# Linear attention and token mixing on one core: a new order table, eps added by TensorE, VectorE work moved away, and 26 products on constant data

## The chip, the cores and the metric

The kernel runs on one core of a Trainium2 chip. The metric is the device time of one execution in microseconds (us). The span of a profile, from the first to the last instruction, is about 2 us shorter. (The profiled execution of the first kernel took 130.3 us, which is 1.8 us over its span; against its median the difference is 3.3 us, as this execution was a quick one.) A run is called slow when it is over 1.5% above the fastest run of the same kernel, otherwise fast; only fast runs are compared. PSUM is the memory that takes TensorE's results here, in banks, and an evacuation is a copy out of it. The granted clock is the share of its full clock that TensorE got, as the profile records it.

## The reference, cut to what matters

```python
# q, k, v: 8 batches x 8 heads x 576 positions x 64, fp32
phi(x) = concat(relu(x) * cos(pos), relu(x) * sin(pos))        # 64 -> 128 features
kv, z  = sum_s phi(k) v^T, sum_s phi(k)                        # per head
x      = phi(q) kv / (phi(q) z + 1e-6)                         # normalization
# x is 8 x 576 x 512 (heads side by side)
W      = (x w_q)(x w_k)^T / 8                                  # 576 x 576 per batch
out    = relu(W x) w_out                                       # 8 x 576 x 512
```

## The kernel before

Every step is a small function. A table, ORDER, lists some 690 words of the form operation.arguments@engine, and the program issues them in that order. Each engine is given its own words in table order. T is TensorE with a PSUM bank, V VectorE (DVE in the profile), A ScalarE (ACT), G GpSimd (POOL), Y SyncE (SP), which issues the transfers.

```python
N_RAW, N_RK, N_KP, N_QD, N_VB, N_QPT, N_KV = 4, 2, 3, 3, 3, 4, 4     # buffers of each kind
N_XS, N_XT, N_WQK, N_WKJ, N_KX, N_MIX, N_OSB = 3, 2, 2, 2, 2, 2, 6
EPS_PE = False
# LD  load half of head pair H (two groups, so four heads) of q, k or v
#         RK, CV, DQ  relu of k, cast of v, doubled relu of q
# MK  kp = rk * cossin (VectorE)                 QK  kv products and q transposes of one group of two heads
# EK  kvs <- PSUM    EQ  qpt <- PSUM * cst       NM  numerators and denominators
def RC(eng, pb, g):
    den = num_view(at["NM", g])[:, :, :, D:D + 1]
    if EPS_PE:
        eng.reciprocal(rec[g % 4], den)
    else:
        eng.tensor_scalar_add(rec[g % 4], den, EPS)
        eng.reciprocal(rec[g % 4], rec[g % 4])
# XN  xs = numerator * rec (the normalization)   XT, WQK, TK, KX, MX  transposes and mixing of one batch
def EO(eng, pb, b, t):                             # evacuation of one output tile
    n, ts = unit_of[b, t]
    copy(eng, osb[n % N_OSB][:, ts.index(t), :], bank1(at["WO", b, t], 0, 4 * DM, FP32))
def ST(eng, pb, b, u, hi):                         # store of one finished output buffer
    ...                                            # (cut: offsets)
    eng.dma_start(dst, osb[n % N_OSB][64 * hi:64 * hi + 64, 0:len(ts), :])
```

There are 32 groups, so 32 normalizations; they serve as landmarks below. WO is the output projection: 36 tiles of four products each.

## Time and profile before

| | before |
|---|---|
| time, median | 131.8 us |
| span of the profile | 128.5 us |
| busy: TensorE, VectorE, ScalarE, GpSimd | 105.4, 106.2, 77.5, 69.4 us |
| end of the 8th, 24th and 32nd normalization | 37.3, 84.6, 108.6 us |
| end of TensorE | 122.2 us |

The ends of normalizations are read from the timeline of VectorE, by counting the multiplications that write xs. Busy shares are averages over stages with different limits, so they have to be read by stretch; the prediction shows these lines. One more line belongs to it, from the waits of SyncE's queue of the kernel before (what it waited for; us in total, times, longest):

```profile
SPq L208 <- ACT rk L193: 8.6, 1, 8.6
```

### The profile page before, as it was taken

The numbers are of one execution on the slowest core, as the hardware profiler recorded it, in microseconds if no ns is written. First come the engines' busy times: TensorE is split into PE (matmuls) and PEld (weight loads), VectorE is DVE, ScalarE is ACT, GpSimd is POOL, SyncE is SP. The second block draws the span as 40 slices with busy tenths as digits, with TensorE's granted clock in tenths as the row PEclk, the third lists the DMA queues.
The fourth block names the chain that finished last, engine by engine and source line by source line (L and its number), as shares of the span: only waits on it lengthen the run. The fifth ranks groups of instructions, "written<-read, shape, count | busy, mean of one in ns | idle before, by whom it ended". The sixth has DMA issues, their size and how long they took to land.

```text
span 128.5 us, 5197 instructions
## 1 busy us (share of the span) xinstructions
PE 105.4 (82%) x2198; PEld 69.4 (54%) x2198; DVE 106.2 (83%) x227; ACT 77.5 (60%) x124; POOL 69.4 (54%) x81
## 2 busy tenths in 40 slices
PE   5935594887879979878999969889999999999900
PEld 2314584847667546566676557364576775543400
DVE  3466999987899999999999896999999998774600
ACT  7125443966396698974976758647977655147110
POOL 7009817098969979995078252389949740020000
PEclk9995558655799999999999999999999999999995
DMA  4999999999999999992068999999998799468793
GB/s 133 276 389 406 391 391 390 331 392 388 389 387 392 391 385 391 390 386 103 5 146 319 303 360 363 340 329 403 384 377 309 176 341 248 107 197 278 186 289 100
DMA packets 20711, 39.40 MB, mean 307 GB/s; under 512 B 3280, under 2 KB 3280, under 8 KB 20688
## 3 DMA queue, kind: packets, MB, share of 16 engines
q1 hardware_dynamic: 19152, 36.32, 81.8%
q10 hardware_dynamic: 1536, 2.75, 6.1%
q8 instruction: 17, 0.28, 0.9%
q14 instruction: 6, 0.05, 0.1%
HBM read 29.62 MB, written 9.44 MB: 304 GB/s over the span
## 4 chain that ended last, share of the span: by engine, by line
DVE 31%; PE 30%; POOL 10%; DMA 8%; SPq 7%; issue 6%; ACT 3%; ACTq 2%; POOLq 0%
DVE kp L232 10%; PE banks L413 10%; DVE xs L309 8%; DVE qpt L279 7%; POOL qd L195 5%; PE banks L260 5%; SPq L208 5%; DMA qf<-in_q_dram 5%; PE banks L269 4%; DMA vf<-in_v_dram 4%; PE banks L292 3%; SPq L430 2%; DVE rec L305 2%; PE banks L343 2%; POOL vb L189 2%
## 5 line engine op out<-in xcount | busy, mean ns | idle before, releaser
L195 POOL TENSOR_SCALAR qd<-qf 128x1152 bf16<-128x1152 f32 x32 | 39.1, 1231 | 12.7 <-DMA qf<-in_q_dram 11.6
L413 PE MATMUL banks<-wo_sb,mix 128*128 128x512 bf16 x144 | 36.0, 380 | 0.0
L232 DVE TENSOR_TENSOR kp<-rk,cossin 128x1152 bf16<-128x1152 bf16 x32 | 29.2, 932 | 1.4 <-POOL rk L195 1.3
L185 ACT COPY osb<-banks 128x512 f32<-128x512 f32 x31 | 18.0, 589 | 12.9 <-PE banks L413 8.2
L309 DVE TENSOR_TENSOR xs<-banks,rec 128x640 bf16<-128x640 f32 x32 | 25.4, 808 | 0.3
L279 DVE TENSOR_TENSOR qpt<-banks,cst 128x1152 bf16<-128x1152 bf16 x32 | 23.9, 746 | 1.1 <-PE banks L269 0.8
L401 ACT ACTIVATE mix<-banks 128x640 bf16<-128x640 f32 (+1 forms) x27 | 17.4, 656 | 8.7 <-PE banks L388 8.1
L260 PE MATMUL banks<-vb,kp 64*128 64x65 bf16 x576 | 16.7, 202 | 3.8 <-DVE kp L232 1.8
L413 PEld LDWEIGHTS <-mix 128*128 128x128 bf16 x144 | 12.1, 98 | 12.5 <-issue 1.4
L292 PE MATMUL banks<-kvs,qpt 128*128 128x65 bf16 x320 | 16.2, 203 | 3.1 <-DVE kvs L187 2.2
L269 PE MATMUL banks<-ident,qd 64*128 64x64 bf16 x576 | 16.2, 201 | 2.2 <-POOL qd L195 2.2
L292 PEld LDWEIGHTS <-qpt 128*128 128x128 bf16 x320 | 13.8, 103 | 7.1 <-DVE qpt L279 2.5
L260 PEld LDWEIGHTS <-kp 64*128 64x128 bf16 x576 | 13.6, 100 | 7.2 <-DVE kp L232 2.5
L193 ACT ACTIVATE rk<-kf 128x576 bf16<-128x576 f32 x15 | 10.1, 684 | 9.1 <-DMA kf<-in_k_dram 8.9
L195 POOL TENSOR_SCALAR rk<-kf 128x576 bf16<-128x576 f32 x14 | 11.3, 812 | 6.6 <-DMA kf<-in_k_dram 2.8
L189 POOL TENSOR_SCALAR vb<-vf 128x576 bf16<-128x576 f32 x17 | 12.3, 726 | 4.6 <-DMA vf<-in_v_dram 3.5
L269 PEld LDWEIGHTS <-qd 64*128 64x128 bf16 x576 | 12.9, 102 | 2.4 <-POOL qd L195 2.4
L185 ACT COPY xT<-banks 128x1280 bf16<-128x1280 bf16 x10 | 12.2, 1225 | 2.9 <-PE banks L326 2.9
L185 ACT CAST vb<-vf 128x576 bf16<-128x576 f32 x14 | 9.4, 673 | 4.7 <-DMA vf<-in_v_dram 4.5
L326 PE MATMUL banks<-ident,xs 64*128 64x64 bf16 x320 | 7.8, 196 | 4.2 <-DVE xs L309 4.1
L189 POOL TENSOR_SCALAR wq<-wqk 64x576 bf16<-64x576 bf16 x4 | 2.8, 712 | 14.9 <-DVE wqk L187 7.8
L343 PE MATMUL banks<-xT,wqk_sb 128*128 128x288 bf16 x64 | 10.1, 306 | 0.7 <-DVE xs L309 0.3
(46 smaller groups left out, 112.8 us busy)
## 6 DMA issues: line engine op xcount, KB each, us to landing
kf<-in_k_dram SPq DMA_DIRECT2D x32, 288.0 KB, 6.0
vf<-in_v_dram SPq DMA_DIRECT2D x32, 288.0 KB, 5.9
qf<-in_q_dram SPq DMA_DIRECT2D x32, 288.0 KB, 6.0
out_dram<-osb SPq DMA_DIRECT2D x21, 256.0 KB, 4.4
out_dram<-osb ACTq DMA_DIRECT2D x9, 256.0 KB, 4.3
out_dram<-osb SPq DMA_DIRECT2D x9, 128.0 KB, 3.4
wo_f<-in_moe_w_out_dram SPq DMA_DIRECT2D x1, 1024.0 KB, 8.3
out_dram<-osb ACTq DMA_DIRECT2D x3, 128.0 KB, 4.0
```

The lines of the kernel that those rows point to most:

```text
L185: A.copy(dst, src)
L189: eng.tensor_scalar(dst, src, 1.0, 1.0, op0=ALU.mult, op1=ALU.mult)
L195: eng.tensor_scalar(dst, src, FMAX, 0.0, op0=ALU.min, op1=ALU.max)
L232: eng.tensor_mul(kp[H % N_KP][:, lo:hi], rk[H % N_RK][:, lo:hi].unsqueeze(3).to_broadcast([P, n, C9, 2, D]), cossin.unsqueeze(1).to_broadc ...
L260: T.matmul(kvp[:, hh, :], kp[H % N_KP][p0:p0 + 64, i, c, :, :], vb[H % N_VB][p0:p0 + 64, i, c, 0:D + 1], start=(c == 0), stop=(c == C9 - 1))
L269: T.transpose(qt[:, hh, c * D:(c + 1) * D], src, ident[p0:p0 + 64, p0:p0 + 64])
L279: eng.tensor_mul(qpt[g % N_QPT][:, :, 1:SLOTS, :], qk_views(at["QK", g])[0].rearrange("f h (c d) -> f h c d", c=C9), cst.unsqueeze(1).to_b ...
L292: T.matmul(nv[:, hh, u, :], qpt[g % N_QPT][:, hh, 2 * u:2 * u + 2, :], kvs[g % N_KV][:, hh, :], start=(u == 0), stop=(u == SC - 1 and not ...
L309: eng.tensor_tensor(xs[b % N_XS][:, :, 2 * pr:2 * pr + 2, :].rearrange("p u h d -> p h u d"), num_view(at["NM", g])[:, :, :, 0:D], rec[g % ...
L343: T.matmul(w[:, nh, :], wqk_sb[:, dmc, :], xT[b % N_XT][:, dmc, D + nh * HS:D + (nh + 1) * HS], start=(dmc == 0), stop=(dmc == NDM - 1))
L401: A.activation(dst, src, AF.Relu, scale=scale_moe)
L413: T.matmul(o, mix[b // 2 % N_MIX][:, dmc, base:base + P], wo_sb[:, dmc, :], start=(dmc == 0), stop=(dmc == NDM - 1))
```

## The change

The intent was to relieve VectorE. The denominators get their eps inside PSUM from a tiny TensorE product, so that 32 VectorE additions go. Thirty of 32 kvs copies go from VectorE to ScalarE, k-relus and v casts from ScalarE and VectorE to GpSimd, ten of the twelve stores that ScalarE issued to SyncE, and more output copies from VectorE to ScalarE. Ten words WU put 26 products on constant data into early gaps of TensorE, to keep its granted clock up. The whole table was rearranged.

```diff
-EPS_PE = False
+EPS_PE = True
+    def WU(eng, pb, n):
+        for _ in range(n):
+            T.matmul(bank1(pb, 0, 2048, FP32), warm[:, 0:P], warm, start=True, stop=True)
 # NM, with EPS_PE, already present in both kernels:
 #     T.matmul(nv[:, hh, :, D], ones_t, eps_t, start=False, stop=True)
 # ORDER: replaced as a whole; number of words by engine, before -> after (cut)
 #   EK  V 32 -> 2,  A 0 -> 30        EO  A 31 -> 36, V 5 -> 0     EMX A 27 -> 30, V 5 -> 2
 #   CV  A 14 -> 6,  G 17 -> 26       RK  A 15 -> 8,  G 14 -> 24, V 3 -> 0
 #   ST  Y 30 -> 40, A 12 -> 2        EX  A 10 -> 11, V 6 -> 5     DW  A 4 -> 7, G 4 -> 1
```

## The prediction

> **What bounds the kernel now.** I read the page first (busy shares, slices, chain), then stretches of the span by engine, the waits, the order of instructions of both kernels, and the minimum and median of single groups.
>
> ```profile
> PE 105.4 (82%) x2198; PEld 69.4 (54%) x2198; DVE 106.2 (83%) x227; ACT 77.5 (60%) x124; POOL 69.4 (54%) x81
> ...
> DVE  3466999987899999999999896999999998774600
> ...
> PEclk9995558655799999999999999999999999999995
> DMA  4999999999999999992068999999998799468793
> ...
> DVE 31%; PE 30%; POOL 10%; DMA 8%; SPq 7%; issue 6%; ACT 3%; ACTq 2%; POOLq 0%
> ```
>
> VectorE (DVE) is full from slice 4 to slice 34, about 12 to 110 us. TensorE is as busy by the count, but its durations include overlapped latency. TensorE's granted clock is down in slices 3 to 10. DMA is full to 57 us, then empty for two slices: one load in SyncE's queue waited 8.6 us for an earlier one's buffer, and the loads and stores behind it waited too. By stretch (columns: PE, PEld, DVE, ACT, POOL busy, clock, DMA share, GB/s):
>
> ```profile
> 0.00:36.00 36.00, 25.35 (x509) 18.25 (x509) 27.94 (x67) 18.60 (x26) 20.80 (x29) 0.72 0.99 353
> 36.00:58.00 22.00, 19.37 (x494) 13.20 (x492) 21.58 (x42) 18.33 (x31) 19.79 (x21) 1.00 1.05 388
> 58.00:72.00 14.00, 13.21 (x314) 9.11 (x315) 13.76 (x34) 10.08 (x17) 6.74 (x7) 1.00 0.51 158
> 72.00:109.00 37.00, 34.28 (x798) 22.74 (x797) 34.41 (x75) 24.73 (x43) 21.40 (x24) 1.00 0.96 329
> 109.00:129.00 20.00, 13.20 (x103) 6.07 (x95) 8.54 (x13) 5.71 (x11) 0.67 (x1) 0.92 0.65 188
> ```
>
> From 36 to 72 us DVE is busy 35.3 of 36 us: it is the bound, even while DMA is empty. Until 36 us DVE, the slow TensorE and the first loads alternate. From 109 us TensorE runs the last projections back to back, and the last stores follow. The last normalization (xs) ends at 108.6 us. The tail after it is 19.9 us.
>
> The rows that I use for costs (busy us, mean ns):
>
> ```profile
> L195 POOL TENSOR_SCALAR qd<-qf 128x1152 bf16<-128x1152 f32 x32 | 39.1, 1231 | 12.7 <-DMA qf<-in_q_dram 11.6 <-PE banks L269 0.3
> L195 POOL TENSOR_SCALAR rk<-kf 128x576 bf16<-128x576 f32 x14 | 11.3, 812 | 6.6 <-DMA kf<-in_k_dram 2.8 <-DVE qpt L279 2.8 <-DVE kp L232 0.7
> L189 POOL TENSOR_SCALAR vb<-vf 128x576 bf16<-128x576 f32 x17 | 12.3, 726 | 4.6 <-DMA vf<-in_v_dram 3.5
> L187 DVE CAST kvs<-banks 128x130 bf16<-128x130 f32 x32 | 8.7, 281 | 1.1 <-ACT xT L185 1.0
> L305 DVE RECIPROCAL rec<-rec 128x10 f32<-128x10 f32 x32 | 6.9, 217 | 1.1
> L304 DVE TENSOR_SCALAR rec<-banks 128x10 f32<-128x10 f32 x32 | 4.9, 153 | 1.0 <-PE banks L292 0.9
> L185 ACT CAST kx<-banks 128x256 bf16<-128x256 f32 x6 | 2.2, 370 | 2.8 <-PE banks L371 2.5
> L453 PE MATMUL banks<-warm 128*128 128x512 bf16 x14 | 5.6, 588 | 1.5 <-DVE warm L451 1.5
> L232 DVE TENSOR_TENSOR kp<-rk,cossin x32: 696/752/1692, 4.1 to 103.0; 128x1152 bf16<-128x1152 bf16 x32
> ```
>
> [...] the clock is 1.00 to 9.9 us, 0.50 to 20.0, 1.00 to 23.3, 0.50 to 33.7, then 1.00[...]; the first low stretch follows a window in which TensorE idled from 7.1 to 8.05 and most of 9 us. [...] the warm-up products started 0.43 us apart and 0.36 us from 6.1 us on. [...] nearly every q-feature product (qpt) now waits for ScalarE. [...] kp takes 0.70 us at least, 1.69 at most, 0.93 on average, though all 32 have one shape.
>
> **The change part by part.**
>
> *VectorE.* Eps: 32 additions go, 4.9 us; the reciprocal reads PSUM itself and stays near 0.22. Moved to ScalarE: 30 of 32 kvs copies, 30/32 of 8.7 = 8.2. Moved elsewhere by the table: 3 k-relus 1.7, a v cast 0.8, 3 mix 2.1, 5 output copies 3.5, 2 kx 0.8, wqk 0.8, wkj 0.3, one xT 0.8. Sum 23.9 us of row time. Neighbours overlap by some 0.06 to 0.09 us, so about 5 of it is not occupancy: 106.2 becomes 82 to 87 us, I take 85.
>
> *ScalarE.* 30 kvs copies at an estimated 0.26 us (from 0.37 for 256 columns and 0.59 for 512) 7.9; 5 output copies 2.9, 3 mix 1.8, 3 q-weight copies 2.0, kx, wqk, wkj, xT 3.0; less 8 v casts 5.4 and 7 k-relus 4.8. Net +7.4: 85 us. Ten store issues of 0.6 us leave its queue.
>
> *GpSimd (POOL).* 9 v casts at 0.73 and 10 k-relus at 0.81, less 3 copies at 0.71: 6.5 + 8.1 - 2.1 = +12.5: 82 us, nearly all ahead of the last normalization.
>
> *TensorE.* At full clock, from steady pieces of the chain: QK 32 x 0.54, NM 32 x 0.31, XT 16 x 0.34, WQK 8 x 0.98, KX 8 x 0.67, MX 32 x 0.17, WO 36 x 0.90, transposes 1.2: 85 us. Added: 64 eps products at about 0.035 (ten NM products take 0.31) 2 us, and 26 constant products, 216 ns each at full clock[...], 0.43 by the trace at half: 5.6 to 11 us, mostly in idle time before about 30 us. If they keep the clock, the second low stretch (10 us) and part of the first go. TensorE pieces there cost half again to twice their later time (18 products 0.67 to 0.68 against 0.46; ten NM 0.73 against 0.47): some 9 us of them are on the chain between 10.8 and 34 us, so 3 us come back, in part the same microseconds as VectorE's.
>
> *By stage.* I add up each engine's row times in table order to the landmarks. Up to the eighth normalization VectorE has 31.7 us before and 21.7 after; it ended at 37.3. After, POOL has most, 22 us; it can start near 5 us because a q load is now second in the queue, so 22 + 5 + about 4 us through TensorE and VectorE is 31 us. A gain of 6. From there to the last normalization: VectorE 76 before (71.3 us elapsed, since row times overlap) and 69 after (62 to 64 without overlap), TensorE 65, ScalarE 63, POOL 58, transfers (at 390 GB/s) 60. Four resources now lie within 10%, so none reaches the 98% that VectorE had; with 65 us at about 96% I get 68 us. Last normalization at 31 + 68 = 99 us against 108.6. In the tail the number of projections falls from 11 to 10 and three ScalarE store issues (3.15 us, in front of the last copy) shrink to one: 19.9 becomes 19. Span 118, and the median time was 3.3 us over the span of the profile: 121.5 us.
>
> **Rivals.** *ScalarE takes VectorE's place as a wait.* A qpt product now starts only after ScalarE has reached and finished the kvs copy, which may stand behind a 0.6 to 1.2 us evacuation in a strict queue. If 30 such waits cost 0.5 us of VectorE time each, 15 of the 21 us come back: about 127. For it: every qpt waits on it. Against: ScalarE is 40% idle, and the table was arranged around it.
> [...] With POOL at 82 us, more kp products collide. Before, 32 x (0.93 - 0.74) = 6 us went that way. If both double, VectorE is at 91 and POOL at 90: last normalization near 104, time 126.
> *The constant products hurt or do nothing.* They have fixed places, so at half clock they are 11 us, and where the gap is not there they delay real work. If the clock stays low until 25 us, I lose the 3 us and 2 or 3 more: 126.
> *Loads.* 39.4 MB at 390 GB/s is 101 us. Another stall like that at 57 us would now be exposed, since TensorE has less backlog: 4 to 6 us.
> *Better than expected.* If DMA alone bounds the middle, the last load lands near 88 us, the last normalization is at 93, and the time is 115.5.
>
> **Range and chances.** Two rivals at once give 129 to 131, none gives 116 to 121. Range 116.5 to 127.5. Faster by over 2% means under 129.2: 0.88. Within 2%: 0.09. Slower: 0.03.
>
> **What would show it.** Right: VectorE busy 82 to 87 and with visible gaps; POOL 80 to 84; ScalarE 83 to 87; clock 1.0 from about 15 us on; eighth normalization at 29 to 33 us, last at 96 to 103; no engine over a third of the chain. Wrong: the largest waits are VectorE's qpt on ScalarE's kvs; kp means over 1.1 us; low clock beyond 20 us; two empty DMA slices again; a tail over 20 us.

## The result, and the profile after

The changed kernel gives the right result and took 137.7 us (median of 4 runs, 136.5 to 139.4) against 131.8 (4 runs). The ratio of the fast runs is 1.042, with a 95% interval of 1.033 to 1.050: it is slower by 4.2%. A ratio here is the mean time of one kernel's fast runs over that of the other's of the same rounds, so it is not quite the ratio of the medians.

First the page of the changed kernel: busy us by engine, the slices of VectorE, the granted clock and DMA, and the chain by engine.

```profile
PE 110.3 (82%) x2288; PEld 69.1 (51%) x2288; DVE 88.4 (65%) x148; ACT 83.6 (62%) x155; POOL 83.3 (62%) x101
...
DVE  2142799997798889999985499987676880202000
PEclk9975799999999999999998699999999998599995
DMA  4999999999999759989999999999945988756883
...
PE 34%; DVE 18%; DMA 14%; POOL 11%; SPq 9%; ACT 5%; issue 3%; ACTq 1%; POOLq 0%
```

VectorE did become light (88 us), the long low clock of the early part is gone (a granted clock of 0.50 only from 8.5 to 15.3 us), and no DMA hole is as deep as before (no slice but the last is under 4 tenths, where one was 0). In the chain VectorE fell from 31% to 18%, and DMA and SyncE's queue (SPq) rose from 15% together to 23%. So the engines changed as intended. Now nearly the same stretches as the prediction shows of before (columns: PE, PEld, DVE, ACT, POOL busy, clock, DMA share, GB/s):

```profile
0.00:36.00 36.00, 27.52 (x583) 17.68 (x583) 23.57 (x47) 16.99 (x28) 29.44 (x44) 0.91 0.99 352
36.00:58.00 22.00, 19.62 (x528) 13.32 (x528) 19.94 (x28) 18.21 (x37) 18.77 (x19) 1.00 0.91 318
58.00:72.00 14.00, 11.93 (x267) 8.04 (x266) 13.11 (x22) 9.34 (x19) 10.83 (x13) 1.00 0.98 330
72.00:109.00 37.00, 34.83 (x775) 22.70 (x775) 27.91 (x49) 26.45 (x52) 23.57 (x26) 0.95 0.89 274
109.00:136.00 27.00, 16.38 (x138) 7.35 (x136) 3.83 (x6) 12.64 (x23) 0.67 (x1) 0.85 0.68 185
```

From 36 to 58 us TensorE is busy 19.6 us, where it was 19.4; from 72 to 109 it is 34.8 against 34.3. TensorE did no more per microsecond although VectorE had air. In the last row VectorE is almost idle (3.8 us) and ScalarE is not (12.6 us): in the kernel before it was 8.5 and 5.7 us.

The landmarks, in us:

| end of | 8th norm. | 15th | 24th | 32nd | TensorE | span |
|---|---|---|---|---|---|---|
| before | 37.3 | 59.1 | 84.6 | 108.6 | 122.2 | 128.5 |
| after | 32.9 | 59.2 | 84.3 | 110.1 | 127.9 | 135.3 |

Each row is one profiled run. How far such landmarks scatter can be read from fast profiled runs whose tables agree up to there: in the kernel before the eighth normalization ended between 35.9 and 37.5 us and the 32nd at 108.6 or 110.4; in the changed one the eighth between 32.9 and 34.8, the 15th between 59.2 and 61.6, the 24th between 83.8 and 85.5. So differences of one or two microseconds in a landmark show nothing.

A lead of 4.4 us at the eighth normalization is gone by the fifteenth. Of the 6.8 us of the spans (the medians differ by 5.9), 5.3 arise behind the last normalization: the tail takes 25.2 us instead of 19.9.

Where the tail loses time is visible by five microseconds. First the kernel before, then the changed one (same columns):

```profile
110.00:115.00 5.00, 5.00 (x41) 2.67 (x39) 3.44 (x6) 2.00 (x4) 0.67 (x1) 1.00 0.45 140
115.00:120.00 5.00, 5.00 (x31) 2.02 (x28) 2.71 (x5) 2.62 (x5) 0.00 (x0) 1.00 0.80 230
```

```profile
110.00:115.00 5.00, 2.56 (x57) 1.39 (x49) 1.22 (x3) 2.02 (x4) 0.00 (x0) 0.93 0.86 245
115.00:120.00 5.00, 4.97 (x29) 2.33 (x29) 0.82 (x1) 3.35 (x7) 0.67 (x1) 0.73 0.79 198
```

TensorE pauses for half of the first stretch, and in the second its clock is granted at 0.73. TensorE's timeline of the changed kernel shows both (start, duration, instructions, idle time before them and its releaser):

```profile
110.60 0.74 PE L373 MATMUL banks<-xs,wkj 128*64 128x256 bf16 x10
113.62 1.23 PE L415 MATMUL banks<-wo_sb,mix 128*128 128x512 bf16 x4 [2.29 <-ACT osb L187]
...
115.68 2.10 PE L345 MATMUL banks<-xT,wqk_sb 128*128 128x288 bf16 x8
```

The pause waits for ScalarE's output copy. Eight products soon after it took 2.10 us, at a granted clock of 0.50 from 114.3 to 117.7 us; the same eight took 1.14 at 111.0 us in the kernel before, at 1.00. What ScalarE waited for is in the waits of the changed kernel, and what was in front of the stores in those of SyncE's queue:

```profile
ACT osb L187 <- DMA out_dram<-osb: 4.9, 2, 4.3
```

```profile
SPq L432 <- ACT mix L403: 13.3, 3, 6.5
SPq L432 <- ACT osb L187: 9.4, 7, 3.3
```

L432 is the store. SyncE stood 22.7 us in front of stores whose data were not ready; counting every wait for ScalarE or VectorE in front of a store it was 24.1 us, against 16.3 in the kernel before and 25.4 in the faster a_st_tail below. So the place of such a wait counts, and not the sum. The longest block, 95.5 to 101.5 us, held older stores behind a store of batch 4; the output buffers, six in all, came free late, and ScalarE waited 4.3 us for one. This suggests a chain, which a_st_tail below tests: store order in SyncE's queue, output buffer, ScalarE, TensorE, clock. Its last link is not a rule: in a_lightload below TensorE paused 2.50 us before the same products, and the clock stayed at 1.00 (the eight took 1.15 us).

### The profile page after: what moved, and what is told of

Read it like the earlier page. It is cut to its first block, busy times and chain, and to the rows that moved or that the text cites. A ratio compares the mean times of both kernels' runs of the same rounds, so it can differ in the third digit from the quotient of the medians.

```text
span 135.3 us, 5328 instructions
## 1 busy us (share of the span) xinstructions
PE 110.3 (82%) x2288; PEld 69.1 (51%) x2288; DVE 88.4 (65%) x148; ACT 83.6 (62%) x155; POOL 83.3 (62%) x101
## 4 chain that ended last, share of the span: by engine, by line
PE 34%; DVE 18%; DMA 14%; POOL 11%; SPq 9%; ACT 5%; issue 3%; ACTq 1%; POOLq 0%
PE banks L415 13%; DVE kp L234 8%; DMA qf<-in_q_dram 6%; SPq L210 5%; DVE xs L311 4%; SPq L432 4%; POOL qd L197 4%; DMA kf<-in_k_dram 4%; DMA out_dram<-osb 4%; DVE qpt L281 4%; PE banks L262 4%; POOL vb L191 3%; POOL rk L197 3%; PE banks L271 3%; PE banks L345 3%
## 5 line engine op out<-in xcount | busy, mean ns | idle before, releaser
L234 DVE TENSOR_TENSOR kp<-rk,cossin 128x1152 bf16<-128x1152 bf16 x32 | 30.9, 989 | 9.6 <-ACT rk L195 7.2
L187 ACT COPY osb<-banks 128x512 f32<-128x512 f32 x36 | 21.2, 591 | 11.6 <-DMA out_dram<-osb 4.9
L191 POOL TENSOR_SCALAR vb<-vf 128x576 bf16<-128x576 f32 x26 | 21.9, 846 | 7.3 <-ACT kx L187 2.8
L403 ACT ACTIVATE mix<-banks 128x512 bf16<-128x512 f32 (+1 forms) x30 | 19.3, 652 | 3.2 <-PE banks L390 3.1
L197 POOL TENSOR_SCALAR rk<-kf 128x576 bf16<-128x576 f32 x24 | 18.3, 767 | 3.8 <-DMA kf<-in_k_dram 1.9
L262 PEld LDWEIGHTS <-kp 64*128 64x128 bf16 x576 | 12.6, 97 | 13.4 <-DVE kp L234 6.2
L187 ACT CAST kvs<-banks 128x130 bf16<-128x130 f32 x30 | 8.1, 271 | 15.9 <-PE banks L271 15.7
L187 ACT COPY xT<-banks 128x1280 bf16<-128x1280 bf16 x11 | 13.5, 1232 | 0.9 <-PE banks L328 0.9
L298 PE MATMUL banks<-eps_t,ones_t 128*128 128x5 bf16 x64 | 10.9, 170 | 0.0
L304 DVE RECIPROCAL rec<-banks 128x10 f32<-128x10 f32 x32 | 6.2, 207 | 6.3 <-PE banks L298 5.7
L191 POOL TENSOR_SCALAR wq<-wqk 64x576 bf16<-64x576 bf16 x1 | 0.7, 666 | 15.0 <-ACT wqk L187 15.0
```

The lines of the kernel that those rows point to most:

```text
L187: A.copy(dst, src)
L191: eng.tensor_scalar(dst, src, 1.0, 1.0, op0=ALU.mult, op1=ALU.mult)
L197: eng.tensor_scalar(dst, src, FMAX, 0.0, op0=ALU.min, op1=ALU.max)
L234: eng.tensor_mul(kp[H % N_KP][:, lo:hi], rk[H % N_RK][:, lo:hi].unsqueeze(3).to_broadcast([P, n, C9, 2, D]), cossin.unsqueeze(1).to_broadc ...
L262: T.matmul(kvp[:, hh, :], kp[H % N_KP][p0:p0 + 64, i, c, :, :], vb[H % N_VB][p0:p0 + 64, i, c, 0:D + 1], start=(c == 0), stop=(c == C9 - 1))
L403: A.activation(dst, src, AF.Relu, scale=scale_moe)
```

## The experiments

Eighteen kernels ran. Ratios are to the kernel before on the same chip; the changed kernel stands at 1.042. Landmarks are of one profiled run each, and the runs were made on several chips, so ratios that lie within each other's intervals are not told apart.

### Single parts of the change, undone or alone

b_eps: the kernel before, with eps by TensorE and nothing else.

```diff
-EPS_PE = False
+EPS_PE = True
```

> The kernel before with the eps part alone (same table). Queue theory (loads and stores in SyncE's queue set the pace as much as VectorE does): VectorE busy falls from 106 to about 101 us, the loads land no earlier, so at most 2% faster: 129 to 132 us. VectorE theory (before is bound by VectorE alone): all 4.9 us come back, about 127. If the 64 eps products hurt on TensorE: slower than 132.5.

Measured: 132.4 us median, ratio 1.001 (0.986 to 1.017). VectorE fell to 101.8 us busy, the 24th normalization was at 85.7. 4.4 us less VectorE work are worth nothing that can be measured here.

a_noeps: the changed kernel with `EPS_PE = False`.

> The changed kernel with eps added on VectorE again, so 64 TensorE products fewer and 32 VectorE additions more. VectorE has slack here, so the reader of the parts expects no change: within 1.5 us of 137.7. If the eps products cost TensorE's backlog 2 us: 135.5. If VectorE still counts: 139 to 141.

Measured: 138.0 us, ratio 1.043 (1.034 to 1.052), VectorE 93.0 us. No effect of the eps shows, for or against.

a_nowu: the changed kernel without the ten WU words.

> The changed kernel without its 26 constant products. If they cost more than they bring (they push back real work, 10 us of TensorE): faster than the changed kernel's 137.7 by 3 us or more. If they keep the clock as meant: the granted clock falls back to 0.5 for some 10 us more between 15 and 35 us and the eighth normalization comes 2 to 4 us later than 32.9 us; the time then rises by 0 to 3 us, less if the loads set the pace after that.

Measured: 138.6 us, ratio 1.044 (1.034 to 1.054). The mean granted clock of its fast runs was 0.92, where fast runs of the changed kernel have up to 0.97 (0.935 in the profiled one). In its profile, which is of a slow run, the page's slices of the granted clock from 17.3 to 38.0 us read 7, 5, 7, 9, 7 and 7 tenths, where the changed kernel's read 9 from 16.9 to 71.0 us. So the clock was higher there with the constant products, but no gain in time shows at the end.

a_ekv: the changed kernel with all kvs copies back on VectorE (30 words EK from @A to @V).

> The changed kernel with the kvs copies back on VectorE (its table otherwise). ScalarE theory (qpt waits on kvs cost VectorE more than the copies did): faster than 137.7 by 2 us or more. If the move was right but worth nothing: VectorE busy 96 to 98 us, time within 1.5 us. If VectorE's relief is worth something even here: 139 to 141.

Measured: 138.4 us, ratio 1.041 (1.026 to 1.055); the profiled run was a slow one. The wait of VectorE for ScalarE's kvs, which the prediction feared most, shows no net effect when it is undone together with the relief.

b_eps_eka: the kernel before with eps by TensorE and all 32 kvs copies on ScalarE, each just ahead of its EQ.

> The kernel before with eps on TensorE and all 32 kvs copies on ScalarE, each ahead of its qpt product, everything else in its old place: VectorE's relief (106 to about 93 us) without GpSimd's new work and without the new table. If VectorE was the bound: 124 to 128 us. If the loads and TensorE's backlog set the end, as the eps part alone suggests: 130 to 133. If waiting for ScalarE costs more than the relief brings: over 134.

Measured: VectorE 96.5 us busy (in the profile of a slow run). Only one run of four was fast, 131.3 us, and not the profiled one; so there is no ratio, and all that can be said is that no large gain shows.

### GpSimd

a_halfpool: the changed kernel with 4 of 9 column blocks of the q copies from the seventh head pair on (wrong result).

```diff
-        relu(eng, qd[...all 9 blocks...], raw["q"][...])
+        nc9 = C9 if H < 6 else 4
+        relu(eng, qd[...the first nc9 blocks...], raw["q"][...])
```

> Wrong result on purpose: the changed kernel, with the q-relu on GpSimd doing 4 of 9 columns from the seventh pair of heads on, some 0.6 us less for each of 20 and wrong numbers. GpSimd theory (GpSimd, 94% busy from 40 to 65 us[...], took VectorE's place as the bound of the middle): GpSimd busy falls by 10 to 12 us, kp's mean falls from 0.99 to under 0.90, the sixteenth normalization comes at 57 to 59 instead of 61.7 us, time 133.5 to 135.5. If the loads or TensorE's backlog set the end: the middle may move, the time stays within 1 us of 137.7.

Measured: GpSimd fell by 11.8 to 71.5 us, kp to a mean of 0.92 us, the 24th normalization to 82.9. (The premise of the expectation was off: in the changed kernel GpSimd was busy 86% from 40 to 65 us, not 94%.) One run was fast, 134.2 us; the three others were 136.6 to 140.3 and slow. That one run is 1.5% over the fast runs before on its chip, so a gain of up to 2.7 points is possible, and the runs don't settle it.

### The stores in SyncE's queue

a_st_early: three stores of batches 0 and 1 that stood in front of loads go further back in the queue.

```diff
 # SyncE's words only
-... ST.0.0.0 ... ST.1.0.0 ... ST.1.0.1 ... ST.0.0.1 ...
+... ST.0.0.0 ST.1.0.0 ST.1.0.1 ST.0.0.1 ...     # all at the place of the last one
```

> The changed kernel with the first three stores (the first projections' results) moved behind the loads that they held up in SyncE's queue. Queue theory: the empty stretch of DMA at 43 to 47.5 us and most of that at 53 to 55 go, loads come 4 to 6 us earlier, the last normalization moves from 110 to about 105, and the time falls by 3 to 5 us to 133 to 135. ScalarE theory (qpt waiting for kvs paces the middle): under 1 us gained.

Measured: 137.9 us, ratio 1.046 (1.035 to 1.057). The block did not vanish but moved: a load now waited 7.1 us for GpSimd's copy, and the transfers stood at a share of 0.21 from 60 to 65 us. (The empty stretches that the expectation names are those of SyncE's queue, which issued nothing from 42.4 to 47.5 us and from 53.2 to 55.3; the transfers of the changed kernel were still at a share of 0.85 in the first of them and fell to 0.05 from 47.5 to 49 us, and from 53 to 55 us they were at 0.96.)

a_st_tail: two stores of batch 4 go behind the older ones that they held up.

```diff
-... ST.4.0.1 ST.3.0.0 ST.2.1.1 ST.4.0.0 ST.3.1.0 ... ST.3.1.1 ST.4.1.1 ...
+... ST.3.0.0 ST.2.1.1 ST.3.1.0 ... ST.3.1.1 ST.4.0.1 ST.4.0.0 ST.4.1.1 ...
```

> The changed kernel with two stores of batch 4 moved behind the older stores that they held up from 95.5 to 101.5 us. Queue theory: ScalarE's 4.3 us wait for an output buffer at 108.7 us goes, the tail after the last normalization falls from 25 to about 20 us, time 133 to 134. If the tail is set by ScalarE doing all evacuations instead: the wait is replaced by others and under 1.5 us is gained.

Measured: 135.4 us, ratio 1.028 (1.016 to 1.040). The 4.3 us wait for an output buffer is gone, the clock stays 1.00 from 75 to 130 us, and the tail of the profiled run is 20.0 us. Its stretches, to compare with the two pairs above:

```profile
110.00:115.00 5.00, 5.00 (x88) 2.69 (x85) 3.57 (x8) 3.66 (x6) 0.00 (x0) 1.00 0.85 212
115.00:120.00 5.00, 5.00 (x43) 2.54 (x43) 0.76 (x1) 4.47 (x9) 0.67 (x1) 1.00 0.41 106
```

From the last normalization to its end TensorE was busy through all of 13.7 us; in the changed kernel it was busy 15.3 of 17.8 us there, in the kernel before 13.6 of 13.6. TensorE's end came down from 127.9 to 126.1 us only, since the last normalization was later, 112.4; 1.2 us of that was there at the 24th (85.5), before the moved stores. So the order of two stores is worth about a third of the loss (1.4 of 4.2 points). The two intervals overlap, but on the same chip the fast runs of a_nowu and a_st_early, which keep the old order at the end, took 136.7 to 138.4 us, and these took 134.3 to 136.2.

### Is it TensorE's backlog?

After these runs the theory was that TensorE's work behind the 24th normalization (21 of 36 output tiles were still to do there, in both tables) sets the end, whatever VectorE does.

b_halfwo and a_halfwo: two of four output products left out for batches 4 to 7 (wrong).

```diff
-        for dmc in range(NDM):
+        nd = 2 if b >= 4 else NDM
+        for dmc in range(nd):
```

> The kernel before with two of the four output-projection products left out for batches 4 to 7 (wrong result on purpose): 18 groups x 2 products x about 0.216 us = 7.8 us less TensorE work, all of it after the 24th normalization. Theory A (the end is set by TensorE's backlog after the 24th normalization, not by VectorE): 24th normalization unchanged at 84 to 86 us, time 124 to 127 us. Theory B (VectorE's queue sets the end even late, as the prediction took it): the time stays at 130 to 132 us.

> The changed kernel with the same cut (wrong result on purpose). Theory A: 24th normalization unchanged at 83 to 86 us, time 130 to 133 us, as the store stall at the end still eats part of the 7.8 us. Theory B (ScalarE's or VectorE's queue sets the end of the changed kernel): 136 to 138 us.

The 0.216 us of a product is also what the trace of the kernel before shows: at a granted clock of 1.00 the output products follow each other every 216 ns (median).

Measured: 130.2 us, ratio 0.992 (0.978 to 1.006), and 138.3 us, ratio 1.050 (1.032 to 1.067; two fast runs, 136.7 and 137.9). This theory fell in its plain form: 7.8 us less TensorE work late give at most 2% to the one and nothing to the other. In b_halfwo TensorE's end came down to 120.7 us only, as the 32nd normalization was no earlier (110.6); from 84 to 110 us TensorE was busy 21.6 of 26 us and idled for the rest. The profile of a_halfwo is a slow run.

a_lightload: half the load bytes of q, k and v from the fifth head pair on (wrong).

```diff
+            n = HC if H < 4 else HC // 2
-            eng.dma_start(raw[t][H % N_RAW][:, i:i + step, :], srcs[t][b][...])
+            eng.dma_start(raw[t][H % N_RAW][:, i:i + step, 0:n], srcs[t][b][..., 0:n])
```

> The changed kernel, loading only half the columns of q, k and v from the fifth head pair on (wrong result on purpose). Theory L (DMA transfers and the blocked queue pace the middle, so that the VectorE time set free cannot be used): 24th normalization falls from 84 us to below 79 us, and the time by 3 us or more, to under 134 us. Rival theory P (GpSimd[...] pace the middle): 24th normalization stays at 83 to 85 us and the time at 136 to 138 us.

Measured: 134.9 us, ratio 1.032 (1.020 to 1.043), 24th normalization at 84.2, so as the rival said there. 10.6 of 39 MB less gave 1.0 points, which the intervals do not tell from none; in the profile they came late. The longest wait of SyncE's queue, on the line of the stores, grew:

```profile
SPq L433 <- ACT mix L404: 17.6, 2, 11.5
```

So the shorter loads did not come earlier here: stores stood in front of them, for 11.5 us at the longest.

b_tail: three last stores of the kernel before go from ScalarE's to SyncE's queue.

```diff
-ST.7.1.1@A ... ST.7.3.0@A ... ST.7.3.1@A
+ST.7.1.1@Y ... ST.7.3.0@Y ... ST.7.3.1@Y
```

> The kernel before with its last three ScalarE-issued stores (batch 7) issued by SyncE instead. In the kernel before ScalarE was issuing these stores from 120.3 to 123.4 us, so that the last evacuation began at 123.5 us though TensorE had ended at 122.2. Theory: the last evacuation starts right after TensorE's end, 0.8 to 1.5 us earlier, time 130.2 to 131.0 us. Rival (the stores' transfers end the kernel whoever issues them): 131.5 to 132 us.

Measured over 6 runs: 132.3 us, ratio 1.009 (0.999 to 1.019). A miss: the last copy did begin right at TensorE's end (124.0 us) and no longer 1.3 us after it, but from there to the end of the span it still took 6.5 us, against 6.3. The copy that waited 3.3 us behind store issues was not what ended the kernel.

### Two limits at once

b_rk10: in the kernel before, the ScalarE copy for which SyncE had waited 8.6 us goes some 7 us earlier (63.6 to 56.4 us in the profiles).

```diff
 # ScalarE's words only
-... EW.2 ... EMX.2.0 RK.10.0 EW.3 ...
+... RK.10.0 EW.2 ... EMX.2.0 EW.3 ...
```

> The kernel before with one instruction moved on ScalarE: the copy of the first half of head pair 10's k (it freed the buffer for which SyncE's queue stood still from 54 to 64 us) goes ahead of batch 3's combined-weight copies, from 63.6 to about 56 us. Theory S (the second half of the kernel before starts from loads that this stall made late): 24th normalization falls from 84 to 86 us to 78 to 82 us, 32nd from 108 to 111 us to 104 to 108 us, time 128 to 130 us. Rival E (the engines are as full as they can be and the stall is absorbed): 24th at 83 to 86 us, time 131 to 133 us.

b_eps_rk10: the same with `EPS_PE = True`.

> The same with the eps by TensorE as well, which relieves VectorE by about 4.5 us (106.2 to 101.8 us busy, run of the eps alone). Theory M (VectorE's relief was masked by the late loads): 1 to 3 us below the same kernel without the eps, 126 to 129 us. Rival: equal to it within 0.7 us.

Measured: 130.5 us median, ratio 1.002 (0.994 to 1.009), and 131.3 us, ratio 0.989 (0.976 to 1.002, two fast runs of six). The stall went (the DMA share from 60 to 70 us rose from 0.43 to 0.98), and the 24th normalization of b_rk10 stayed at 84.4 us. So the stall was absorbed. The second kernel is the fastest correct one tried by its ratio, but its interval reaches past 1, so it is not shown to beat the kernel before.

b_all and a_all: half the load bytes and half of all output products (wrong).

> The kernel before with half the load bytes from the fifth head pair on and half of all output-projection products (36 groups x 2 x about 0.216 us = 15.6 us less TensorE work), both wrong on purpose. Theory C (TensorE and the loads limit the second half side by side, so that relieving one alone gave 0 to 1 us): 24th normalization below 82 us, time 118 to 125 us, bounded then by VectorE's 106 us and its waits. Rival D (neither limits, a chain of waits between the in-order queues does): 127 to 131 us.

> The changed kernel with the same two cuts. Theory C: the VectorE work saved shows once both others are relieved, so that it falls below the kernel before with the same cuts: 24th normalization below 80 us, time 115 to 122 us. Theory D or a new order table that is itself slower: 130 to 137 us, above the kernel before with the same cuts.

Measured: b_all 126.1 us, ratio 0.960 (0.948 to 0.972). a_all had one fast run, 129.1 us, and three slow of 132.2 to 132.6; the five fast runs before on this chip were 129.6 to 131.5, so no ratio is given. Theory C was half right: the two cuts together give the kernel before 4%, where half of the products of four batches had given nothing that could be told from noise. Half of all products alone, and the loads alone, were not run on this kernel, so it is not shown that it takes both. But the 24th normalization came down only to 83.1 and 82.5 us, and the changed kernel stayed behind the other. VectorE's relief does not show even here. The last normalization of the two is at the same time, 107.0 and 107.3 us; what separates the profiled runs (both slow) is the tail, 17.8 against 23.1 us.

### The middle and the tail of the changed kernel

a_mid: half the load bytes, the short q copies of a_halfpool, and ST.0.0.0 and ST.1.0.0 issued by ScalarE right behind their copies.

> The changed kernel with the feed of its middle relieved in three ways at once: half the load bytes from the fifth head pair on, about half of GpSimd's q copies from the seventh pair on (both wrong on purpose), and the two stores that stood in front of loads in SyncE's queue issued by ScalarE right behind their own copies. Theory F (buffers, loads and GpSimd together pace the middle; the run with the loads alone left an 11.5 us block in that queue): 24th normalization falls from 84 us to below 79 us. Rival L (the handovers between TensorE, ScalarE and VectorE, each in strict order, pace it): 24th normalization at 81 to 85 us. The tail is untouched by this run, so the time should follow the 24th normalization, less 1 to 3 us for the tail's TensorE work.

Measured: 133.2 us, ratio 1.022 (1.007 to 1.037; only two of the seven runs before on this chip were fast), 24th normalization at 80.9. This lies just below the range of theory L and above that of theory F. It is the largest move of this landmark by any run. The feed did pace part of the stretch, some 3.4 us (2.9 below the lowest of the tables that agree with the changed one up to there), but a further store (ST.1.0.1) now held SyncE for 10.6 us, so the feed was not wholly free. From 58 to 84 us TensorE went from 23.1 us busy to nearly all of it. First the changed kernel, then a_mid:

```profile
58.00:84.00 26.00, 23.13 (x490) 15.10 (x488) 21.53 (x37) 17.38 (x35) 19.29 (x23) 0.93 0.98 314
```

```profile
58.00:84.00 26.00, 25.13 (x581) 16.98 (x583) 23.63 (x43) 20.02 (x40) 16.07 (x22) 1.00 0.76 211
```

With the feed relieved, TensorE is nearly full there at once: 25.1 of 26 us. Part of the difference is this one profile of the changed kernel: TensorE waited 1.95 us for a v cast of GpSimd at 70.9 us and then had a granted clock of 0.50 from 73.3 to 76.8 us, which a_st_tail, with the same table there, did not have.

a_tail_v: a_st_tail, and 14 evacuations of the end, nearly all of batches 6 and 7, on the engines of the kernel before.

```diff
-EO.5.1@A EX.14@A EW.7@A EMX.6.2@A EKX.7@A EO.6.0@A EMX.7.0@A EMX.7.3@A EO.7.1@A EO.7.3@A EO.7.4@A
+EO.5.1@V EX.14@V EW.7@V EMX.6.2@V EKX.7@V EO.6.0@V EMX.7.0@V EMX.7.3@V EO.7.1@V EO.7.3@V EO.7.4@V
-EMX.6.0@V EMX.7.1@V EMX.6.1@A   ST.7.3.0@A
+EMX.6.0@A EMX.7.1@A EMX.6.1@V   ST.7.3.0@Y
```

> The changed kernel with the two stores moved as in the run that took 135.42 us, and with the evacuations of batches 6 and 7 on the engines that they had in the kernel before (14 of them; 11 go from ScalarE to the idle VectorE, 3 the other way). Theory T (ScalarE alone evacuating makes the tail long): TensorE's end falls from 125 to 123 us or less and the time to 132 to 133.7 us. Rival (TensorE's own backlog sets the tail once the store is out of the way): TensorE's end at 124.5 to 126 us, time 134.5 to 136 us.

Measured: 132.9 us, ratio 1.018 (1.000 to 1.037), correct. The time is the one that theory T expected; TensorE's end, 124.6 us in the profile, came 1.6 us earlier than in a_st_tail, which is in the range of the rival. Its stretches, to compare with the two shown of the tail above:

```profile
110.00:115.00 5.00, 4.95 (x76) 2.85 (x76) 3.97 (x6) 2.17 (x5) 0.00 (x0) 1.00 0.57 152
115.00:120.00 5.00, 4.95 (x40) 2.01 (x39) 2.85 (x5) 2.75 (x6) 0.67 (x1) 1.00 0.44 111
```

VectorE and ScalarE share the tail as in the kernel before, TensorE runs on, and the clock holds at 1.00. But TensorE ran on in a_st_tail too, with VectorE nearly idle, and from the last normalization to TensorE's end both took 13.7 us. The 1.6 us by which TensorE's end came earlier were there at the 24th normalization already (83.8 against 85.5), up to which the two tables agree. So by the profiles the rival is right: with the stores out of the way TensorE's own work sets the tail, and that ScalarE evacuates alone is not shown to cost anything. The time agrees with theory T, but its interval is wide (two fast runs before), it overlaps that of a_st_tail, and the two were not run side by side. Both edits together take 2.3 of the 4.2 points, of which the store order has 1.4; the rest may be scatter. (The expectation miscounts: of the 14 evacuations twelve go to VectorE and two to ScalarE; and one store went to SyncE with them.)

## Why the prediction was wrong

The engines did what it said: VectorE 88.4 us busy (82 to 87 was said), ScalarE 83.6 (83 to 87), GpSimd 83.3 (80 to 84). VectorE is 1.4 us over its range, and kp accounts for it: its mean rose from 0.93 to 0.99 us, 32 x 0.057 = 1.8 us. The early clock came as said, low only from 8.5 to 15.3 us.

Three smaller readings in it were off and do not change the outcome. The clock was not 1.00 from the start: warm-up products 0.43 us apart until 6.1 us are what the prediction itself takes for half clock (from there one started 0.36 us and the next 0.22 us after the one before). In the changed kernel products of the same 512 columns followed each other every 0.40 to 0.43 us at a granted clock of 0.50 (74.3 to 75.5 us), and constant ones every 0.22 us at 1.00 (16.3 to 18.0 us). The hole in the transfers lay from 59 to 65 us (a DMA share of 0.03). And of the 3.3 us added to the span 1.5 are no such difference: the profiled execution of the kernel before was a quick one.

**The first failed step was what bounds the kernel.** The prediction read "From 36 to 72 us DVE is busy 35.3 of 36 us: it is the bound". In the line beside it TensorE was busy 32.6 of the same 36 us. From the 8th to the 32nd normalization, first before and then changed:

```profile
37.30:108.60 71.30, 65.50 (x1536) 44.00 (x1537) 68.05 (x147) 51.44 (x86) 46.92 (x51) 1.00 0.90 313
32.90:110.10 77.20, 70.58 (x1646) 46.64 (x1646) 63.98 (x101) 56.52 (x108) 55.63 (x59) 0.98 0.92 301
```

TensorE was busy 92% of the first stretch and 91% of the second. VectorE's share fell from 95% to 83%, and TensorE's did not move: the relief of VectorE let TensorE do no more per microsecond. The single runs agree: eps alone, eps undone and kvs copies undone each show no effect within their intervals, of about 1 to 1.5% to either side. So it is shown that VectorE alone was not the bound. What limits in its place is argued: that TensorE's work and the feed (loads, buffers, GpSimd, the in-order queue of SyncE) limit side by side fits the runs with several cuts. The loads alone left the 24th normalization where it was; three reliefs of the feed took it from 84.3 to 80.9 us and then TensorE was nearly full.

**The term that was mis-sized** is the share in "65 us at about 96%" for the middle, which gave 68 us and came out at 77.2. The 65 us can be checked with the steady costs that the prediction lists for TensorE. Summed with these, as an estimate, the words between the two landmarks are 60.1 us before and 64.1 after (one QK, one WO and two MX more, one TK less, 48 eps products, 1.7 us, and three constant ones, 0.6 us). So the work was sized rightly, and the share was 83%, where the kernel before already had 84%. The step from 84 to 96% was to come from VectorE's relief, and it did not come. (Busy time is larger, 65.5 and 70.6 us, as it counts every product up to its modelled end: an output product has a mean of 380 ns in the kernel before, and the next one starts 216 ns after it; by either count the share stays.) Against the kernel before the stretch is 5.9 us longer: the added 4.0 us of work take 4.7 at a share of 84%, and the granted clock of 0.50 from 73.3 to 76.8 us of the profiled run at most 1.7; this too is an estimate.

**The eighth normalization at 31 us** was right as a number (32.9) and wrong in what was drawn from it. A part of the lead was work put off behind the landmark: one QK, one KX and four MX, 0.54 + 0.67 + 4 x 0.17 = 1.9 us; the rest was gone by the 15th. A landmark compares two orders only if the work left behind it is the same.

**The tail, 19 us in the prediction, took 25.2.** The prediction counted projections and store issues on ScalarE. It did not ask what the store in front of SyncE's queue waits for. a_st_tail shows this: with two stores moved the tail is 20.0 us, as in the kernel before. A tail over 20 us was named as a sign of being wrong.

**The rivals.** "Another stall like that ... would now be exposed" came true, but in the stores: 6 us in the queue, 4.3 us on ScalarE, 2.3 us on TensorE, then a granted clock of 0.50 from 114.3 to 117.7 us. All 30 qpt products whose kvs ScalarE copies began after the end of that copy, 0.03 to 3.98 us; ScalarE as a wait came to 6.0 us of VectorE time, with no cost to the end that a_ekv shows. The longer kp, which the prediction puts down to collisions with GpSimd, cost VectorE 1.8 us more, where 6 were feared. In each of the two traces twelve of the 32 kp took 0.86 to 1.70 us, all of them while GpSimd was at work; those without GpSimd beside them, 12 and 8, took 0.69 to 0.76, as did some with it; why is not shown. In a_halfpool, with 11.8 us less of GpSimd, the mean fell from 0.99 to 0.92 us. The constant products cost nothing that shows.

**What stays open.** With the store order mended 2.8 points are left (1.6 to 4.0), with both edits of the tail 1.8 (0 to 3.7). As the tails of these profiled runs, 20.0 and 20.5 us, are then about as long as before (19.9), the rest should lie ahead of the last normalization, and no run takes it apart. In fast profiled runs with the full work the stretch from the 24th to the 32nd normalization took 25.8 to 28.0 us in changed kernels and 24.0 to 25.4 in kernels before; with half the load bytes the changed ones took 24.8 and 24.3, so the loads may have a part in it. Nor is it shown which single handover paces the changed kernel from the 8th to the 15th normalization: this stretch took 25.9 to 27.8 us in all its fast profiled runs, 21.8 to 24.3 in those of kernels before. And the new order is not separated from the moves between engines: only b_eps_eka tried such moves, and a part of them, in the old order.

## What to carry to other kernels

An engine at 98% is the bound only if the next one has room (here TensorE was busy 32.6 of the 36 us in which VectorE was busy 35.3): relieve it on paper, and take from the runner-up's own share in that stretch the most that can be won. Before a landmark is compared, look how far it scatters between runs whose code agrees up to there. And in a queue that issues in the order of its table, put a store only where its data will be ready: in SyncE's queue here all that stood behind a store, loads and older stores alike, waited with it, for 6.5 us in the changed kernel and 11.5 us in a_lightload.
